# Float32 weighted sums and state products split over two halves of the array's columns, under an order found by a longer search

## The chip, the cores and the metric

The kernel runs on one core of a Trainium2 chip. The metric is the device time of one execution in microseconds (us); lower is better. Engines are named as in the profile: PE is TensorE (its matmuls), PEld its weight loads, DVE is VectorE, ACT is ScalarE, POOL is GpSimd, SP issues most of the DMAs.

## The reference

Attention with a decaying state over 768 tokens, for 4 batches and 8 heads of width 40, then two dense layers with a leaky activation, then three dense layers whose elementwise maximum goes through a last one:

```python
for t in range(S):
    m_new = np.maximum(f_gate[:, :, t] + m, i_gate[:, :, t])
    f_stab = np.exp(f_gate[:, :, t] + m - m_new)
    i_stab = np.exp(i_gate[:, :, t] - m_new)
    C = f_stab * C + i_stab * outer(v_t, k_t)
    n = f_stab * n + i_stab * k_t
    y[:, :, t] = sigmoid(o_t) * (C @ q_t) / np.maximum(np.abs(n @ q_t), 1.0)
...
h = x @ w_in                                   # 3072 x 320 by 320 x 2048
x = (np.maximum(h, 0) + alpha * np.minimum(h, 0)) @ w_out
h = np.maximum(np.maximum(x @ w1, x @ w2), x @ w3)      # 320 x 768 each
return h @ w_out2
```

All data are float32.

## The kernel before

The attention goes by tiles of 128 tokens, 24 in all (`ORDER`). A tile has four products on PE: the scores (`ps`), the weighted sum of the values (`pov`), the product of the queries with the state (`piv`), and the state's own update (`pcv` in `state`, from the 64 columns `kv` and the weighted values `vw`). The state C has 40 rows (on partitions) and 41 columns for each head; the 41st carries n.

Two forms exist. `attention32` works in float32 and serves the 8 tiles for which `whole(p)` holds: six of batch 0 and the first of batches 1 and 2. They are in the first three chunks of three tiles. All others go through `attention`, in pieces of float16; only their state update is in float32. A float32 matmul of the program appears in the profile as two PE instructions. The profile's names: `va` and `db` (or `hl`, where the weights `db` lie in that buffer) are the operands of `pov`; `C` and `q`, `ph` or `hl` (buffers of queries) are those of `piv`; `vw` and `kv` those of the state update.

The dense layers go by 8 chunks of 384 tokens. A unit of the first layer (`m1_unit`) is 8 matmuls of 384 columns (`xT`, `wi`), of the second (`m2_tile`) 12 of 320 (`g`, `wo`) in each of 4 pieces per tile, of the three layers (`m3_unit`) 8 of 384 (`x2T` or `xT`, `wq`), of the last (`m4_tile`) 9 of 320 (`h`, `wp`) in each of 2 pieces. The results are drained from the 8 PSUM banks and split into two float16 parts by DVE, ACT and POOL: after a unit of the first layer ACT writes `d`, DVE `gf`, then two of the three engines write `g`. The weights come as 64-bit floats and are taken apart, measured and converted on chip: their norms are matmuls of 128x128 on PE (from buffer `g` for `w_in`, `wo` and `x2T` for `w_out`, `h` for w1 to w3 in three batches of 15, `wp` for the last), each after a step of DVE that assembles the float32 values, and then the largest goes through `TENSOR_REDUCE dm`, a matmul with `ones`, some steps on DVE, and a conversion of each weight tile (`wo<-wo,sbo` on DVE is the second half of one).

Nothing is issued in the order in which it is written. `Sched` records all operations, and `order` plans them: `forward` simulates the engines by a table of costs (`cost`) and takes on each free engine the ready operation with the earliest due time; `backward` gives new due times from a plan. Where a plan leaves PE idle, it may put in filler matmuls (`ones`, 128x256), which keep the engine active. An operation written with `either` may go to either of two engines. Each engine then runs its list strictly in the planned order, so that an operation that waits holds up all that stands behind it on its engine.

In the code below, line 641 (of before) issues all planned operations, and line 635 the fillers.

Of the kernel before, what the change touches and what calls it, by code (L numbers as in the profile page):

```python
# [51 lines left out]
BY_DMA = 3  # L52

LAG = 4

AFTER = (0, 1, 2, 3)
ROW0 = [sum(CHUNKS[:j]) for j in range(NCH + 1)]
# [85 lines left out]
class Sched:  # L143
# [95 lines left out]
    def cost(self, op, meth, kw, outs, ins):  # L239
        n = 1  # L240
        for x in (ins[0] if meth == "tensor_reduce" else outs[0]).shape[1:]:
            n *= x
        psum = any(a.space == bass.MemoryType.PSUM for a in ins + outs)
        if op.eng == "pe":
            f32 = ins[0].dtype == F32
            wide = kw["lhsT"].shape[1] > 64 if meth == "matmul" else False

            pair = 2 if f32 and ins[0].shape[0] <= 64 else 1
            busy = n * ((4 if meth == "matmul" else 2) if f32 else 1) / 2.4
            if f32 and meth == "matmul":  # L250
                dur = max(busy / pair + 3.5, (214.0 if wide else 107.0) / pair)
            else:
                dur = max(busy + 2.5, 25.0)

            op.weight = (op.weight * op.dur + busy * ins[0].shape[0] / 128.0) / (op.dur + dur)
            op.dur += dur
            lhs = kw["lhsT"] if meth == "matmul" else ins[0]
            op.shape = (ins[0].shape[0] <= 64, lhs.shape[1] <= 64 if meth == "matmul" else False)
        elif op.eng == "act":
            op.dur += n / 1.2 + (60 if psum else 93)  # L260
            if outs[0].shape[0] == 64:
                op.dur += 112
            op.dur += 93 * ("accum_out" in kw)
            op.dur += 93 * sum(hasattr(kw.get(k), "ap") for k in ("scale", "bias"))
        elif op.eng == "dve":
            rate = 0.96
            if meth == "reciprocal":
                rate /= 8
            elif meth in ("tensor_scalar", "tensor_copy", "memset") and not psum:
                rate *= 2  # L270
            if meth == "tensor_tensor_scan":
                rate /= 2
            op.dur += n / rate + 67
            if outs[0].shape[0] == 64 and not psum:
                op.dur += 112
            op.dur += 63 * any(hasattr(kw.get(k), "ap") for k in ("scalar", "scalar1", "scalar2"))
        elif op.eng == "pool":
            op.dur += 100 + ({"affine_select": 1.4, "memset": 1.0}.get(meth, 2.0)) * n
        else:
            b = outs[0]  # L280
            size = SIZE[b.dtype]
            for x in b.shape:
                size *= x
            run = min(self.run(a) for a in (b, ins[0]))
            inside = bass.MemoryType.DRAM not in (b.space, ins[0].space)
            if meth == "dma_start_transpose":
                op.dur += 1290.0
            else:
                op.dur += (590.0 if run < 2048 else 790.0) if inside else 610.0 if b.shape[0] == 64 else 420.0
            n, m = (next((d[1] for d in a.ap if d[1] > 1), 1) for a in (b, ins[0]))  # L290
            k = max(k for k in range(1, 17) if n % k == 0 and m % k == 0)
            slow = run >= 2048 and not (self.level(ins[0]) and self.level(b))
            op.tail = size / run * (self.DMA_EACH + run * (self.DMA_APART if slow else self.DMA_BYTE)) / k
            if meth == "dma_start_transpose":
                op.tail = size / 150.0
# [49 lines left out]
    def order(self):  # L345
        ops = self.ops
        for op in ops:
            op.succ = []
        for i, op in enumerate(ops):
            for d in op.deps:  # L350
                ops[d].succ.append(i)
        best = None
        dice = random.Random(0)

        def walk(due, rounds):
            nonlocal best
            won = None
            for _ in range(rounds):
                plan = self.forward(due)
                if plan is None:  # L360
                    due = [x * 1.01 for x in due]
                    continue
                start, ends, fill = plan
                span = max(ends)
                late = self.backward(start, ends)
                if best is None or span < best[0]:
                    best = (span, start, ends, due, fill, [op.eng for op in ops])
                if won is None or span < won[0]:
                    won = (span, late)
                due = late  # L370
            return won

        from_ = min((w for w in (walk(self.deadlines(*x), ROUNDS) for x in STARTS) if w), key=lambda w: w[0])
        for k in range(SHAKES):
            wide = (12000.0, 4000.0, 1500.0)[k % 3]
            won = walk([x + dice.uniform(-wide, wide) for x in from_[1]], 4)
            if won and won[0] < from_[0]:
                from_ = won
        _, start, ends, due, (self.fill, owner), engs = best
        for bank, n in owner.items():  # L380
            bank.tile = self.tiles[n]
        for op, e in zip(ops, engs):
            if op.forms:
                op.eng, op.calls, op.dur, op.table, op.port = next(f for f in op.forms if f[0] == e)
        self.plan = (start, ends, due)
        return sorted(range(len(ops)), key=lambda i: (start[i], i))
# [266 lines left out]
def kernel(  # L653
# [300 lines left out]
    def attention32(n, xt, t0):  # L954

        b, c = ORDER[n]
        i = b * CT + c
        last = c == CT - 1
        if n % 3 == 0:
            sigmoids(n // 3)  # L960
        t = r_q()
        qt, kt = t[:, 0:4], t[:, 4:8]
        for hh in range(2):
            sp.dma_start(
                out=t[64 * hh:64 * hh + 40].rearrange("p (s h) t -> p s (h t)", s=2),
                in_=qk[i, :, :, 4 * hh:4 * hh + 4, :].rearrange("s p h t -> p s (h t)"),
            )
        gt, db, gm = decays(i)
        kv = r_kv()
        sp.dma_start(out=kv[:, :, 0:DM], in_=tok[i, :, 1:3, :])  # L970
        va = r_va()
        copy(va[:, :, 0:D], kv[:, 1, 0:DM].rearrange("p (h d) -> p h d", d=D))
        ps = [bank("s").rearrange("p (h t) -> p h t", h=4) for _ in range(2)]
        sc.unit()
        for h in range(4):
            for hh in range(2):
                p = slice(64 * hh, 64 * hh + 40)
                pe.matmul(out=ps[hh][:, h, :], lhsT=kt[p, h, :], rhs=qt[p, h, :], start=True, stop=True)
        sc.end()
        for hh in range(2):  # L980
            sl = slice(4 * hh, 4 * hh + 4)
            dve.tensor_tensor(out=db[:, sl], in0=ps[hh], in1=db[:, sl], op=ALU.mult)
        num = r_num() if c else None
        if c:
            cn = carry["C", b]
            piv = [half(bank("a")) for _ in range(2)]
            sc.unit()
            for h in range(4):
                for hh in range(2):
                    p = slice(64 * hh, 64 * hh + 40)  # L990
                    pe.matmul(out=piv[hh][:, h], lhsT=qt[p, h, :], rhs=cn[p, h, :], start=True, stop=True)
            sc.end()
            sc.after(carry["pov"])
            carry["piv"] = len(sc.ops) - 1
            for hh in range(2):
                sl = slice(4 * hh, 4 * hh + 4)
                dve.tensor_tensor(
                    out=num[:, sl], in0=piv[hh], in1=bc(gt[1][:, sl].unsqueeze(2), [128, 4, VA]), op=ALU.mult
                )
        if not last:  # L1000
            vw = r_vw()
            combine(vw, va, bc(gt[2].unsqueeze(2), [128, H, VA]), ALU.mult)
            state(b, c, kv, vw, gm)
        pov = per_head(bank("a"))
        sc.unit()
        for h in range(H):
            pe.matmul(out=pov[:, h], lhsT=db[:, h, :], rhs=va[:, h], start=True, stop=True)
        sc.end()
        if c:
            sc.after(carry["piv"])  # L1010
        carry["pov"] = len(sc.ops) - 1
        if c:
            dve.tensor_tensor(out=num, in0=pov, in1=num, op=ALU.add)
        else:
            num = pov
        finish(n, num, 1.0, xt, t0)
# [513 lines left out]
    for j in range(NCH + LAG):  # L1530
        k = j - LAG
# [63 lines left out]
    (3.0, 30000.0, 1.1),  # L1595
)
ROUNDS = 8
SHAKES = 60
OFFSET = 950.0
STAY = 0.37  # L1600
EARLY = 100000.0
# [50 lines left out]
```

## Time and profile before

| | |
|---|---|
| median of 3 runs | 705.4 us (704.2 to 707.29) |
| the profiled execution: time | 704.88 us |
| its span, first to last instruction | 703.1 us |
| PE busy | 677.5 us, 96% of the span |
| DVE busy | 480.1 us, 68% |
| ACT busy | 392.0 us, 56% |
| mean granted clock of PE | 0.98 of full speed |

A PE that is busy is not a PE at its peak: at half clock it is as busy and does half as much, and the fillers count as well. DVE's 68% is a mean over stretches that differ, so the rows further down are taken by stretch.

### The profile page before, as it was taken

The page shows a single profiled execution, that of the slowest core. Times are in us where ns is not written, and L with a number is a line of the kernel's source. Part 1 is how long each engine was busy: PE and PEld are TensorE (multiplying, and loading weights), DVE is VectorE, ACT ScalarE, POOL GpSimd, SP SyncE. Part 2 cuts the span into 40 slices and gives each one's busy share as a digit, 9 for nine tenths or more (in the row PEclk, how much of TensorE's full clock was granted, in tenths as well). Part 3 has the DMA queues.
Part 4 walks back from the last instruction along what each step waited for, and adds up shares of the span by engine and source line. Part 5 has one row for each costly group of instructions (what it writes and reads, how often), then busy time and mean ns, then how long its engine had stood idle before and what let it go on. Part 6 is the DMA issues. An engine that isn't in the chain of part 4 may idle for free.

```text
span 703.1 us, 14517 instructions
## 1 busy us (share of the span) xinstructions
PE 677.5 (96%) x5353; PEld 456.1 (65%) x5353; DVE 480.1 (68%) x1221; ACT 392.0 (56%) x941; POOL 135.7 (19%) x162
## 2 busy tenths in 40 slices
PE   8898999999999898999999999999999999999998
PEld 5665767667666566666666666666666666666665
DVE  6989889987898989999499835882284214242332
ACT  4778778796986886987376614741253122222222
POOL 1103341131550520442034101410030000000000
PEclk9889799999999999999999999999999999999999
DMA  7978657698744456862624432212101210002000
GB/s 192 281 252 286 220 162 203 203 262 200 206 105 142 139 141 188 268 202 77 184 78 125 128 76 68 70 35 54 52 2 35 35 57 1 29 8 55 10 20 29
DMA packets 81856, 85.76 MB, mean 122 GB/s; under 512 B 38386, under 2 KB 65978, under 8 KB 81786
## 3 DMA queue, kind: packets, MB, share of 16 engines
q1 hardware_dynamic: 81450, 84.77, 42.9%
q8 instruction: 42, 0.69, 0.4%
q14 instruction: 28, 0.23, 0.1%
q10 hardware_dynamic: 336, 0.07, 0.0%
HBM read 59.35 MB, written 8.75 MB: 97 GB/s over the span
## 4 chain that ended last, share of the span: by engine, by line
PE 53%; DVE 5%; ACT 3%; DMA 2%; issue 1%; SPq 1%; ACTq 0%; DVEq 0%
PE bank L641 53%; DVE wq L641 1%; DMA raw<-w 1%; DMA raw<-tok 1%; ACT xs L641 1%; DVE xs L641 1%; SPq L641 1%; DVE g L641 1%; DVE gf L641 0%; ACT wq L641 0%; ACT g L641 0%; ACT raw L641 0%; ACT d L641 0%; DVE num L641 0%; ACT db L641 0%
## 5 line engine op out<-in xcount | busy, mean ns | idle before, releaser
L641 PE MATMUL bank<-xT,wi 128*128 128x384 f16 x1024 | 176.4, 328 | 2.5 <-DVE gf L641 1.6
L641 PE MATMUL bank<-wo,g 128*128 128x320 f16 x1152 | 164.4, 299 | 0.4 <-DVE db L641 0.3
L641 PEld LDWEIGHTS <-wq 128*128 128x128 f16 x1152 | 111.6, 98 | 74.4 <-DVE wq L641 1.6
L641 PEld LDWEIGHTS <-g 128*128 128x128 f16 (+1 forms) x1192 | 114.8, 99 | 47.2 <-DVE g L641 2.4
L641 PEld LDWEIGHTS <-wi 128*128 128x128 f16 x1024 | 98.2, 98 | 65.1 <-issue 5.0
L641 PE MATMUL bank<-x2T,wq 128*128 128x384 f16 x720 | 123.7, 328 | 1.9 <-DVE wq L641 1.2
L641 POOL TENSOR_TENSOR g<-gf,g 128x384 f16<-128x384 f32 x58 | 57.3, 988 | 212.9 <-ACT g L641 140.7
L641 DVE TENSOR_TENSOR mv<-bank,mv 128x384 f32<-128x384 f32 x96 | 53.0, 552 | 62.1 <-PE bank L641 61.7
L641 DVE SCALAR_TENSOR_TENSOR gf<-d,al,bank 128x384 f32<-128x384 f32 x128 | 76.4, 604 | 9.7 <-ACT d L641 8.9
L641 ACT ACTIVATE h<-mv 128x384 f16<-128x384 f32 x46 | 24.0, 522 | 96.1 <-DVE mv L641 96.1
L641 ACT ACTIVATE d<-bank 128x384 f32<-128x384 f32 x128 | 60.7, 479 | 19.3 <-PE bank L641 17.4
L641 PE MATMUL bank<-xT,wq 128*128 128x384 f16 x432 | 71.2, 326 | 0.0
L641 ACT ACTIVATE g<-gf 128x384 f16<-128x384 f32 x104 | 53.6, 518 | 22.2 <-DVE gf L641 21.9
L641 PE MATMUL bank<-wp,h 128*128 128x320 f16 x432 | 61.6, 299 | 0.0
L641 PEld LDWEIGHTS <-h 128*128 128x128 f16 (+1 forms) x477 | 45.7, 98 | 21.2 <-DVE h L641 3.6
L641 ACT ACTIVATE db<-db,gtok 128x128 f32<-128x128 f32 x168 | 54.9, 390 | 0.5 <-POOL db L641 0.4
L641 POOL TENSOR_SCALAR_AFFINE_SELECT db<-db 128x512 f32<-128x512 f32 x42 | 35.0, 849 | 67.5 <-ACT gm L641 52.2
L641 ACT ACTIVATE raw<-raw 128x960 f32<-128x960 f32 (+8 forms) x71 | 44.9, 665 | 2.3 <-DMA raw<-w 1.1
L641 DVE TENSOR_TENSOR g<-gf,g 128x384 f16<-128x384 f32 x70 | 40.8, 588 | 5.8 <-ACT g L641 4.9
L641 POOL TENSOR_TENSOR h<-mv,h 128x384 f16<-128x384 f32 x10 | 9.3, 927 | 167.9 <-ACT h L641 166.1
L641 DVE TENSOR_SCALAR sx<-sx 128x1 int32<-128x1 int32 x48 | 7.1, 147 | 44.6 <-ACT xs L641 44.4
L641 DVE TENSOR_TENSOR h<-mv,h 128x384 f16<-128x384 f32 x38 | 21.1, 556 | 18.1 <-ACT h L641 17.9
(209 smaller groups left out, 797.9 us busy)
## 6 DMA issues: line engine op xcount, KB each, us to landing
db<-ddr SPq DMA_DIRECT2D x21, 512.0 KB
kv<-tok SPq DMA_DIRECT2D x24, 320.0 KB
raw<-tok SPq DMA_DIRECT2D x15, 480.0 KB
q<-qk SPq DMA_DIRECT2D x38, 160.0 KB
raw<-w SPq DMA_DIRECT2D x9, 512.0 KB
qs<-hl SPq DMA_DIRECT2D x48, 80.0 KB
x2d<-xs SPq DMA_DIRECT2D x24, 160.0 KB
ks<-hl SPq DMA_DIRECT2D x48, 80.0 KB
```

The source lines that it names most:

```text
L641: getattr(e, meth)(**{k: v.on(v.bank.tile) if isinstance(v, View) else v for k, v in kw.items()})
```

## The change

In `attention32`, each matmul of `piv` and `pov`, which had 128 columns of weights (the tile's 128 tokens), becomes two of 64 columns, for tokens 0 to 63 and 64 to 127, one after the other. Their results go to partitions 0 to 63 and 64 to 127 of the same bank. The state update already had this form (64 columns, the two halves in turn) and is left alone, as are the scores.

In the planner, `cost` gets another price for float32 matmuls (with 64 columns of weights the price is now for halves that run beside each other; this is also the state update's, of 20 tiles). `order` compares plans by their span plus a fifth of the mean start, and each of now 200 further attempts moves the due times of the best plan so far within one stretch, for one round, instead of 60 attempts over the whole program for four rounds.

```diff
+HALVES = (slice(0, 64), slice(64, 128))
...
-            pair = 2 if f32 and ins[0].shape[0] <= 64 else 1
+            pair = 1
+            if f32 and meth == "matmul":
+                pair = (1 + (ins[0].shape[0] <= 64)) * (1 + (kw["lhsT"].shape[1] <= 64))
...
-                dur = max(busy / pair + 3.5, (214.0 if wide else 107.0) / pair)
+                dur = max(busy / pair + 3.5, kw["lhsT"].shape[1] * 1.67 / pair + 6.0)
...
-                if best is None or span < best[0]:
+                worth = span + 0.2 * sum(start) / len(start)
+                if best is None or worth < best[0]:
...
-            wide = (12000.0, 4000.0, 1500.0)[k % 3]
-            won = walk([x + dice.uniform(-wide, wide) for x in from_[1]], 4)
+            won = walk([x + dice.uniform(-wide, wide) if a <= x < b else x for x in from_[1]], 1)
...
-                for hh in range(2):
-                    p = slice(64 * hh, 64 * hh + 40)
-                    pe.matmul(out=piv[hh][:, h], lhsT=qt[p, h, :], rhs=cn[p, h, :], start=True, stop=True)
+                for t in HALVES:
+                    for hh in range(2):
+                        p = slice(64 * hh, 64 * hh + 40)
+                        pe.matmul(out=piv[hh][t, h], lhsT=qt[p, h, t], rhs=cn[p, h, :], start=True, stop=True)
...
-            pe.matmul(out=pov[:, h], lhsT=db[:, h, :], rhs=va[:, h], start=True, stop=True)
+            for t in HALVES:
+                pe.matmul(out=pov[t, h], lhsT=db[:, h, t], rhs=va[:, h], start=True, stop=True)
...
-SHAKES = 60
+SHAKES = 200
```

The new plan moves instructions on every engine. (Line 647 of the changed kernel issues what line 641 did, and its line 641 the fillers.) Three places show how.

PE, around the norm of `w_out` (`dm`, `ones` 128x4) and the first unit of the second layer (`wo`, `g`); first before, from the last of the norms that this step waits for:

```order
L641 MATMUL bank_67<-x2T 128x128
L641 MATMUL bank_69<-va_138,db_135 128x41 x8
L641 MATMUL bank_66<-vw_141,kv_133 64x41 x8
L641 MATMUL bank_63<-ph_142 128x128
...
L641 MATMUL bank_64<-C_145,ph_142 128x41
...
L641 LDWEIGHTS ones
L641 MATMUL bank_67<-dm_164,ones 128x4
L641 LDWEIGHTS wi_90
L641 MATMUL bank_69<-xT_110,wi_90 128x384
```

And the same place in the changed kernel, to the first unit of the second layer:

```order
L647 MATMUL bank_64<-x2T 128x128
L647 LDWEIGHTS ones
L647 MATMUL bank_64<-dm_164,ones 128x4
L641 LDWEIGHTS ones
L641 MATMUL bank_69<-ones 128x256
...
L647 MATMUL bank_69<-vw_141,kv_134 64x41 x8
L647 MATMUL bank_70<-va_138,db_136 64x41 x16
...
L647 LDWEIGHTS g_105
L647 MATMUL bank_66<-wo_92,g_105 128x320
```

The four float32 groups that stood between the norms and the step `dm`, `ones` now stand ahead of the norms; behind that step, 13 fillers stand where four units of the first layer (`xT`, `wi`) were mixed with the float32 groups.

DVE, just ahead of the reduction that this step needs, first before:

```order
L641 CAST g_107<-gf_118 128x384
L641 SCALAR_TENSOR_TENSOR gf_119<-d_117,al_75,bank_69 128x384
L641 TENSOR_TENSOR db_135<-bank_66,db_135 128x512
L641 TENSOR_TENSOR db_135<-bank_63,db_135 128x512
L641 TENSOR_TENSOR num_143<-bank_68,gtok 128x164
L641 TENSOR_TENSOR num_143<-bank_64,gtok 128x164
L641 TENSOR_REDUCE dm_164<-bank_67 128x4
```

and then in the changed kernel:

```order
L647 SCALAR_TENSOR_TENSOR gf_119<-d_117,al_75,bank_70 128x384
L647 TENSOR_TENSOR C_145<-bank_63,C_145 128x164
L647 TENSOR_SCALAR dn_152<-num_143 128x8
...
L647 TENSOR_TENSOR g_108<-gf_119,g_108 128x384
L647 TENSOR_TENSOR y_144<-num_143,dn_152 128x320
L647 TENSOR_REDUCE dm_164<-bank_64 128x4
```

The reduction was DVE's 177th instruction and is now its 190th: steps of the first layer's units and of one attention tile (`num`, `dn`, `y`) have moved ahead of it.

PE, in the second batch of norms for w1 to w3 (`h`), where before seven of them stand together behind a weighted sum:

```order
L641 MATMUL bank_67<-vh_139,ph_142 128x41
L641 LDWEIGHTS h_109
L641 MATMUL bank_68<-h_109 128x128
...
L641 LDWEIGHTS wq
L641 MATMUL bank_69<-x2T,wq 128x384
```

and in the changed kernel the last of the same batch:

```order
L647 LDWEIGHTS h_109
L647 MATMUL bank_65<-h_109 128x128
L647 LDWEIGHTS wi_89
L647 MATMUL bank_64<-xT_111,wi_89 128x384
...
L647 LDWEIGHTS h_109
L647 MATMUL bank_65<-h_109 128x128
L647 LDWEIGHTS wq
L647 MATMUL bank_68<-x2T,wq 128x384
```

In the second and third batch the norms now stand one by one, each with a unit or half a unit of other work behind it.

## Rows read from the trace of the kernel before

**Rows 1.** The page: busy time of each engine, share of the span, instructions.

```profile
PE 677.5 (96%) x5353; PEld 456.1 (65%) x5353; DVE 480.1 (68%) x1221; ACT 392.0 (56%) x941; POOL 135.7 (19%) x162
```

**Rows 2.** Busy time by stretch: from:to, length, then each engine, clock, DMA.

```profile
0.00:98.10 98.10, 85.16 (x730) 63.67 (x730) 82.68 (x219) 70.02 (x154) 19.94 (x38) 0.88 0.78 235
98.10:353.10 255.00, 245.84 (x2132) 167.09 (x2131) 221.99 (x593) 199.26 (x510) 76.12 (x83) 0.99 0.64 180
353.10:703.10 350.00, 346.50 (x2493) 225.30 (x2492) 175.47 (x411) 122.76 (x279) 39.68 (x42) 1.00 0.18 48
```

**Rows 3.** The chain that ended last: start, us, what.

```profile
352.62 0.48 DVE dm L641
353.14 346.51 PE bank L641 x2493
```

**Rows 4.** Timeline of PE, 60 to 99 us: start, length, instruction.

```profile
62.32 1.09 PE L641 MATMUL bank<-C,ph 40*128 40x41 f32 x16
63.34 1.47 PE L641 MATMUL bank<-xT,wi 128*128 128x384 f16 x8
64.74 0.67 PE L641 MATMUL bank<-vw,kv 128*64 128x41 f32 x16
65.34 1.98 PE L641 MATMUL bank<-va,db 128*128 128x41 f32 x16
67.15 0.23 PE L641 MATMUL bank<-wo 128*128 128x128 bf16 x1
67.22 1.46 PE L641 MATMUL bank<-xT,wi 128*128 128x384 f16 x8
68.52 0.22 PE L641 MATMUL bank<-wo 128*128 128x128 bf16 x1
...
79.85 3.58 PE L641 MATMUL bank<-va,db 128*128 128x41 f32 x16
83.36 1.08 PE L641 MATMUL bank<-vw,kv 128*64 128x41 f32 x16
...
86.24 1.77 PE L641 MATMUL bank<-C,ph 40*128 40x41 f32 x16
87.95 0.19 PE L641 MATMUL bank<-dm,ones 128*128 128x4 bf16 x1
...
98.10 0.58 PE L641 MATMUL bank<-wo,g 128*128 128x320 f16 x3
```

**Rows 5.** Busy time in two stretches of low granted clock, columns as in rows 2.

```profile
77.50:91.50 14.00, 14.00 (x113) 12.04 (x113) 9.87 (x27) 9.60 (x26) 4.84 (x7) 0.51 0.51 151
...
240.00:256.00 16.00, 13.67 (x118) 8.62 (x116) 13.76 (x34) 14.00 (x42) 5.11 (x6) 0.89 0.60 158
```

**Rows 6.** Timeline of DVE between the reduction and the first converted weights.

```profile
80.09 0.69 DVE L641 TENSOR_REDUCE dm<-bank 128x4 bf16<-128x512 f32 x1 [0.42 <-PE bank L641]
...
88.33 0.15 DVE L641 TENSOR_SCALAR xm<-bank 128x4 int32<-128x4 int32 x1
...
91.67 0.33 DVE L641 TENSOR_TENSOR C<-bank,C 128x164 f32<-128x164 f32 x1 [0.80 <-PE bank L641]
...
94.77 0.50 DVE L641 TENSOR_TENSOR num<-bank,num 128x328 f32<-128x328 f32 x1 [0.61 <-PE bank L641]
...
96.15 0.87 DVE L641 SCALAR_TENSOR_TENSOR wo<-wo,sbo,wo 128x640 f16<-128x640 f32 x1
```

**Rows 7.** Timeline of PE at the second batch of norms.

```profile
241.59 0.76 PE L641 MATMUL bank<-vh,ph 128*128 128x41 f16 x24
242.20 0.27 PE L641 MATMUL bank<-h 128*128 128x128 bf16 x2
243.47 0.23 PE L641 MATMUL bank<-h 128*128 128x128 bf16 x1 [0.99 <-DVE h L641]
245.03 0.61 PE L641 MATMUL bank<-h 128*128 128x128 bf16 x4 [1.34 <-DVE h L641]
```

**Rows 8.** The state update's weight loads: count, busy us, mean ns, idle.

```profile
L641 PEld LDWEIGHTS bank<-vw,kv 128*64 128x64 f32 x320 | 11.6, 145 | 6.3 <-issue 3.3 <-DVE sx L641 1.1 <-POOL vw L641 0.7
```

More of the change, by code (lines that the diff above doesn't have):

```diff
@@ L245, in cost @@
             f32 = ins[0].dtype == F32
-            wide = kw["lhsT"].shape[1] > 64 if meth == "matmul" else False
-            pair = 2 if f32 and ins[0].shape[0] <= 64 else 1
+            pair = 1
+            if f32 and meth == "matmul":
+                pair = (1 + (ins[0].shape[0] <= 64)) * (1 + (kw["lhsT"].shape[1] <= 64))
             busy = n * ((4 if meth == "matmul" else 2) if f32 else 1) / 2.4
             if f32 and meth == "matmul":
-                dur = max(busy / pair + 3.5, (214.0 if wide else 107.0) / pair)
+                dur = max(busy / pair + 3.5, kw["lhsT"].shape[1] * 1.67 / pair + 6.0)
             else:
@@ L365, in walk @@
                 late = self.backward(start, ends)
-                if best is None or span < best[0]:
-                    best = (span, start, ends, due, fill, [op.eng for op in ops])
-                if won is None or span < won[0]:
-                    won = (span, late)
+                worth = span + 0.2 * sum(start) / len(start)
+                if best is None or worth < best[0]:
+                    best = (worth, start, ends, due, fill, [op.eng for op in ops])
+                if won is None or worth < won[0]:
+                    won = (worth, due)
                 due = late
@@ L374, in order @@
         for k in range(SHAKES):
-            wide = (12000.0, 4000.0, 1500.0)[k % 3]
-            won = walk([x + dice.uniform(-wide, wide) for x in from_[1]], 4)
+            end = max(from_[1])
+            a = dice.uniform(-0.05, 0.95) * end
+            b = a + dice.choice((20000.0, 60000.0, 150000.0, 800000.0))
+            wide = dice.choice((500.0, 1500.0, 4000.0, 12000.0))
+            won = walk([x + dice.uniform(-wide, wide) if a <= x < b else x for x in from_[1]], 1)
             if won and won[0] < from_[0]:
```

## The prediction

> **What bounds the kernel now.** I read the busy times first, then the chain that ended last, then the same busy times by stretch, cut where the chain and PE's timeline say that the limit changes. PE is busy for 96% of the span [rows 1], which looks like one bound for the whole program. The chain says otherwise: from 353.1 us on it is PE alone, 2493 matmuls in 346.5 us without a break, and just before that it runs over DVE, whose step `dm` is the measure of the last weights [rows 3]. So I divide the span in three [rows 2].
>
> Stage A, 0 to 98.1 us, ends with the first unit of the second layer [rows 4]. PE is busy for 85.2 of 98.1 us, part of it with fillers and part at half clock; DVE is busy for 82.7. Stage B, 98.1 to 353.1 us, ends with the matmul behind that last `dm`. PE is busy for 245.8 of 255.0 us and idle for 9.2, DVE is busy for 222.0 and ACT for 199.3: PE is the nearest bound, DVE a close second. Stage C, 350 us, is PE's alone; DVE is busy for half of it, and nothing that DVE, ACT or the DMAs save there can show. The sum is made against the profiled execution: 704.9 us, of which the span is 703.1; that is 0.5 us below the median of 705.4, and I forecast on the execution's scale. About 0.5%, 3.5 us, is what a measurement of this kernel can tell from no change: below 701.9 I call it faster, above 708.9 slower.
>
> **The matmuls that are split.** One `pov` is 16 instructions in 65.34 to 67.15 us, 1.81 us at full clock. The new one is 32 instructions of the very form of the state update (128 rows, 64 columns of weights, 41 moving columns, float32, halves in turn), which takes 16 instructions from 64.74 to 65.34, 0.60 us [rows 4]. Twice that is 1.20 us, so each `pov` gives 0.61 us. `piv` is 16 instructions in 1.02 us (62.32 to 63.34). With 40 rows and 64 columns four pieces of the array could work at once, a form that the trace does not have. At the pitch of the state update, 37.5 ns, 32 instructions would be 1.20 us, a loss of 0.18; at the shortest pitch I find, 24 float16 matmuls of the same 41 columns in 0.61 us, 25.4 ns each [rows 7], they would be 0.81 us, a gain of 0.21. I take nothing, as the middle.
>
> Counted in the order, 6 of the 8 `pov` and 4 of the 5 `piv` stand in stage A before and after the change; 2 and 1 stand in stage B. None is in stage C. So of the whole 8 x 0.61 = 4.9 us only 1.2 us lies where PE is the bound; the other 3.7 us lie in stage A and count only if what ends stage A comes earlier. The price of a change of form, when PE goes from whole columns to halves, is seen at the state update: the unit ahead of it takes 1.40 us (63.34 to 64.74) where another takes 1.30 (67.22 to 68.52), so 0.10 us. The order has 12 more such changes, all of them in stage A; in stages B and C the count stays at 32. They are hidden with the rest of stage A; without that cover they would cost 1.2 us.
>
> **A rule that speaks against the split.** The 16 weight loads and matmuls of a state update start 37.5 ns apart though a load takes 145 ns on average [rows 4, 8], so loads and matmuls of the two column halves do overlap. The Trainium skill, "TensorE: Matmul & The Clock Gate", section "The mechanism", says that a weight load overlaps with running matmuls only when its row group differs; the two halves here have the same rows. By that rule the split would gain nothing; the trace's state update disagrees, and I go by the trace.
>
> **The end of stage A.** The first unit of the second layer waits for converted weights, and these for a chain: norms on PE, the reduction on DVE, a matmul with `ones` on PE, steps on DVE, the conversion. Before, the reduction starts at 80.09 us [rows 6], but the matmul behind it only at 87.95, since 8.1 us of float32 groups stand ahead of it on PE (79.85 to 87.95), all of them at half clock [rows 4, 5]: a `pov` takes 3.51 us there, a state update 1.01. DVE goes on at 88.33, and converts the second weight tile from 96.15 to 97.02 [rows 6]; PE starts the unit at 98.10.
>
> In the new order nothing stands between the norms and the matmul with `ones`, so these 8 us of waiting are gone. Instead 13 more instructions stand ahead of the reduction on DVE. At the stage's mean, 82.7 us for 219 [rows 2], they are 4.9 us; by their kinds (five `gf`, three `g` and small ones) I count 5.9. The reduction then starts at 86.0, ends at 86.7, and DVE goes on some 0.4 us later at 87.1, 1.2 us earlier than before. From there to the conversion DVE took 7.8 us, 1.4 of it waiting for PE's slow float32 groups (0.80 and 0.61 [rows 6]); with half of that wait gone, the conversion starts 1.9 us earlier. PE has 13 fillers and 5 us of float32 work to do meanwhile, so it is ready. I take 1.9 us off stage A. The bounds: a gain of 6.9 us, if all that the low clock took from 77.5 to 91.5 us comes back (14.0 us at a mean of 0.51 of full speed [rows 5]); and a loss of 1.5 us, if DVE waits in front of the reduction for the attention steps that now stand there, as long as the 1.4 us that it waited behind it.
>
> **Stage B and C.** Counted by the order, two units of the first layer (2.6 us) move from C to B, and the two split `pov` take 1.2 us off B; the two stages together lose 1.2 us of PE work. In B, PE's clock fell to half at the second batch of norms: two waits of 0.99 and 1.34 us for DVE within 3 us, among single matmuls [rows 7], and of the 16 us there 11% of the clock was lost [rows 5], 1.8 us of work. In the new order the norms of that batch and the next stand one by one between units, so such waits no longer fall together. I take the 1.8 us off, and leave the 9.2 us of idle time as it is: the new order has other waits in the place of these, and which is larger no row tells. The bounds are 0 and all of 9.2 us.
>
> SP issues as many DMAs as before, no wait of PE in stage B is for a DMA, and the state update, whose price in the planner halves, is not itself changed: there I expect nothing.
>
> The sum: -1.9 (A) -1.2 (split, B) -1.8 (clock, B) = -4.9, so 704.9 - 4.9 = 700.0 us.
>
> **Rivals.** *DVE holds up stage B (slower).* Between the conversion at the end of stage A and the last `dm`, DVE has 607 instructions where it had 596. The 11 more are wide ones, splits and scalings that went to ACT or POOL before; by kind I count 6.2 us (4.1 at the mean of 222.0 us for 593 [rows 2]). PE has 1.4 us more there. If DVE keeps its share of waiting, stage B grows with it: 255.0 x (6.2 / 222.0) = 7.1 us. Less the 1.9 of A and the 2.6 us that left C, that is +2.6: 707.5 us; it is slower than before from 4.5 us of added DVE time that finds no gap. Against it: DVE is idle for 33 us of stage B, and PE, not DVE, is nearest to full. Slower by more than 0.5% takes a further 1.4 us.
>
> *The waits of stage B go (much faster).* If the longer search fits DVE's work so that PE hardly waits, the 9.2 us go too: 700.0 - 9.2 = 690.8. For it speaks the new price of the state update: a head cost 107 ns in the old plan and 59 in the new one, where it takes 75 (0.60 us for 8 heads [rows 4]), so PE ran ahead of the old plan, into waits, and falls behind the new one. Against it: the planner meant the old stage B to be nearly free of waits as well (it placed two fillers there, as now), and the 9.2 us came all the same.
>
> *Nothing but the two splits counts.* The gate of stage A comes no earlier (the 5.9 us on DVE are matched by waits), and the clock falls elsewhere instead: 704.9 - 1.2 = 703.7.
>
> *The halves do not overlap.* 32 loads at 145 ns [rows 8] are 4.6 us where a `pov` took 1.81: 2.8 us each, 5.7 in stage B alone and up to 22.6 in all, 711 to 727 us. Only a difference between `pov` and the state update that I do not see could bring it; this is what the rule of the skill above comes to.
>
> **How the numbers follow.** 0.38 for the forecast (its own range 697 to 703), 0.17 for the waits that go (690 to 697), 0.24 for nothing but the splits (703 to 706), 0.19 for DVE (706 to 711), 0.02 for halves that do not overlap. The likeliest is 700.0. Leaving out some 0.08 at the low end and 0.10 at the high end gives 693 to 708.5. Faster by over 0.5%: 0.17 and 0.31 of the forecast's 0.38 below 701.9, so 0.48. Slower: 0.02 and 0.15 of DVE's 0.19, so 0.17. The rest, 0.35, is no change that can be told.
>
> **What would show it.** A `pov` of 32 instructions in 1.2 us, a `piv` near 1.0. The reduction `dm` 128x4 at about 86 us, the matmul behind it at once, the first unit of the second layer at about 96. Between that and the last `dm`, PE's idle time: 9 us bears the forecast out, 14 and more, with waits for DVE, the rival; a granted clock of 1.00 from 240 us on. From the last `dm` to the end, 2.6 us less than 350. Wrong would make it above all a stretch of half clock in the new stage A or B that the old order did not have, since 13 fillers in a row show that the plan itself has PE waiting there.

## The result and the profile after

The changed kernel takes 695.96 us (695.4 to 696.97, 4 runs) where the kernel before, on the same chip, took 705.15: a ratio of 0.9867, 95% interval [0.9842, 0.9893], so 9.2 us less. Single executions far off the others of their kernel (2093 and 2401 us below, 714 and 728 us of the kernel before) are in no ratio of this document. The changed kernel's profiled execution has a span of 694.1 us, 9.0 less than 703.1. Cut at the same two places as before (the first `wo`, `g`, and the matmul behind the last `dm` 128x3), its busy times by stretch are these; columns as in [rows 2]:

```profile
0.00:91.10 91.10, 72.89 (x886) 51.17 (x887) 79.68 (x213) 68.00 (x152) 18.45 (x37) 0.94 0.85 248
91.10:345.50 254.40, 246.72 (x2193) 166.80 (x2191) 227.16 (x611) 199.89 (x517) 67.02 (x76) 0.99 0.65 183
345.50:694.10 348.60, 344.32 (x2483) 223.89 (x2480) 172.48 (x405) 120.95 (x273) 40.81 (x45) 1.00 0.17 48
```

Beside [rows 2], stage A is 7.0 us shorter (98.1 to 91.1), stage B 0.6, stage C 1.4. So 7.0 of the 9.0 us, over three quarters, lie in the stage where the forecast had put 1.9 of 4.9. The granted clock of A rose from 0.88 to 0.94. Before, it stood at half (1.2 of 2.4 GHz) from 29.9 us for 10.2 us, from 77.7 for 13.7, and in B from 244.9 for 3.4. Now, in this execution, it falls five times, but never for more than 3.4 us; the same view, cut at these falls and at the place of [rows 5]:

```profile
22.00:25.50 3.50, 3.30 (x26) 2.66 (x27) 2.10 (x8) 2.19 (x6) 0.15 (x1) 0.51 1.04 281
39.20:42.60 3.40, 2.98 (x18) 2.04 (x18) 3.35 (x14) 2.59 (x7) 0.00 (x0) 0.50 0.97 312
83.50:86.90 3.40, 3.26 (x22) 2.18 (x21) 2.23 (x11) 3.40 (x9) 0.00 (x0) 0.51 0.74 212
158.60:162.00 3.40, 3.40 (x32) 2.45 (x29) 3.19 (x10) 3.28 (x8) 0.00 (x0) 0.51 0.42 108
240.00:256.00 16.00, 15.28 (x125) 10.72 (x126) 15.62 (x39) 13.87 (x41) 4.04 (x5) 1.00 0.62 156
315.60:319.00 3.40, 3.40 (x17) 1.66 (x14) 2.88 (x10) 1.56 (x6) 0.00 (x0) 0.51 0.56 195
```

The fall at 240 to 256 us is gone, as forecast; those at 158.6 and 315.6 are new. In all of stage A the clock stands at half for 10.2 us where it was 23.9. PE's timeline around the end of stage A, which answers to [rows 4] (start, length, instruction):

```profile
74.17 0.68 PE L647 MATMUL bank<-C,q 40*64 40x41 f32 x32
74.78 0.23 PE L647 MATMUL bank<-wo 128*128 128x128 bf16 x1
...
77.65 1.13 PE L647 MATMUL bank<-va,db 128*64 128x41 f32 x32
78.72 0.23 PE L647 MATMUL bank<-wo 128*128 128x128 bf16 x1
...
80.90 0.68 PE L647 MATMUL bank<-C,ph 40*64 40x41 f32 x32
81.51 0.35 PE L647 MATMUL bank<-x2T 128*128 128x128 bf16 x3
83.64 0.17 PE L647 MATMUL bank<-dm,ones 128*128 128x4 bf16 x1 [1.78 <-DVE dm L647]
83.66 2.94 PE L641 MATMUL bank<-ones 128*128 128x256 bf16 x13
...
91.10 1.11 PE L647 MATMUL bank<-wo,g 128*128 128x320 f16 x7
```

From its start to the start of what follows, a split `pov` takes 1.07 us (77.65 to 78.72) for its 32 instructions, a split `piv` 0.61 (74.17 to 74.78): both shorter than forecast (1.20 and 1.02). The float32 groups that stood behind the norms now run at full clock, and ahead of the last of these. Behind the step `dm`, `ones` come the 13 fillers, as the order showed. DVE's timeline, which answers to [rows 6]:

```profile
82.91 0.68 DVE L647 TENSOR_REDUCE dm<-bank 128x4 bf16<-128x512 f32 x1
...
87.42 0.33 DVE L647 TENSOR_TENSOR C<-bank,C 128x164 f32<-128x164 f32 x1 [1.66 <-PE bank L647]
```

The reduction starts at 82.91 us and the matmul behind it 0.73 us later (before: 80.09, and 7.86 later). From the reduction to the first unit of the second layer it is now 8.2 us, and was 18.0.

One more row of the kernel before is needed, its busy time from the wait at 75.98 us to the end of stage A; columns as in [rows 2]:

```profile
75.98:98.10 22.12, 22.12 (x196) 18.51 (x196) 17.21 (x53) 15.46 (x39) 6.49 (x9) 0.69 0.53 157
```

PE is busy for all of these 22.12 us, at 0.69 of full speed, and DVE for 17.21. So the first unit of the second layer did not wait for the converted weights: it began when PE was through with what stood ahead of it. There, time taken off PE's work brings the end of stage A forward, for as long as PE does not come to wait.

### The profile page after: what moved, and what is told of

Read it like the earlier page. It is cut to its first block, busy times and chain, and to the rows that moved or that the text cites. A ratio compares the mean times of both kernels' runs of the same rounds, so it can differ in the third digit from the quotient of the medians.

```text
span 694.1 us, 14964 instructions
## 1 busy us (share of the span) xinstructions
PE 663.9 (96%) x5558; PEld 441.9 (64%) x5558; DVE 479.3 (69%) x1227; ACT 388.8 (56%) x940; POOL 126.3 (18%) x157
## 4 chain that ended last, share of the span: by engine, by line
PE 57%; DVE 5%; ACT 1%; issue 1%; DVEq 0%; ACTq 0%
PE bank L647 57%; DVE gf L647 1%; DVE db L647 1%; DVE ph L647 0%; DVE g L647 0%; ACT db L647 0%; DVE wp L647 0%; DVE num L647 0%; DVE y L647 0%; DVE h L647 0%; DVE dn L647 0%; DVE vh L647 0%; DVE wq L647 0%; DVE xs L647 0%; ACT xs L647 0%
## 5 line engine op out<-in xcount | busy, mean ns | idle before, releaser
L647 PE MATMUL bank<-xT,wi 128*128 128x384 f16 x1024 | 174.6, 326 | 2.3 <-DVE db L647 1.4
L647 POOL TENSOR_TENSOR g<-gf,g 128x384 f16<-128x384 f32 x54 | 52.9, 984 | 206.7 <-ACT g L647 144.6
L647 ACT ACTIVATE g<-gf 128x384 f16<-128x384 f32 x111 | 57.2, 519 | 16.3 <-DVE gf L647 15.7
L647 DVE TENSOR_TENSOR g<-gf,g 128x384 f16<-128x384 f32 x74 | 43.8, 600 | 10.2 <-ACT g L647 9.4
L647 ACT ACTIVATE raw<-raw 128x512 f32<-128x512 f32 (+8 forms) x70 | 44.6, 655 | 4.0 <-DMA raw<-tok 2.6
L647 POOL TENSOR_TENSOR h<-mv,h 128x384 f16<-128x384 f32 x15 | 13.7, 913 | 178.3 <-ACT h L647 173.6
L647 POOL TENSOR_SCALAR_AFFINE_SELECT db<-db 128x512 f32<-128x512 f32 x42 | 31.1, 761 | 80.3 <-ACT gm L647 57.8
L647 ACT ACTIVATE mv<-bank 128x384 f32<-128x384 f32 x35 | 17.0, 487 | 30.1 <-PE bank L647 30.1
L647 ACT ACTIVATE xs<-bank 128x320 f16<-128x320 f32 x24 | 10.3, 429 | 40.7 <-PE bank L647 40.4
```

The lines of the kernel that those rows point to most:

```text
L647: getattr(e, meth)(**{k: v.on(v.bank.tile) if isinstance(v, View) else v for k, v in kw.items()})
```

## The experiments

Two theories stood against each other. *The order* (P in the expectations): stage A is shorter since the new plan puts the float32 groups ahead of the norms; the split is hidden there. *The split and the clock* (S): stage A is shorter since split groups end sooner or no longer run at half clock, whatever the order. A third question is what in the planner made the plan better: the price, the longer search, or chance. The kernels ran in three groups, each on a chip of its own, where the kernel before had medians of 706.6 to 708.4 us; so ratios to it are compared, and stages from the one profiled execution of each. The profiled execution of the kernel before took 704.9 us, 1.7 to 3.5 us less than these medians, so stages show less gain than ratios.

**The changed kernel again** (no edit), for the spread.

> The changed kernel itself, unchanged, beside the next three on one chip, so that they can be held against it: ratio to before 0.987, as in the first comparison (0.984 to 0.989); stage A 91, stage B 254, stage C 349 us.

Measured: 696.57 us, ratio 0.9849 [0.9818, 0.9880]. Stages A, B and C are 92.8, 251.4 and 349.1 us where the first profile has 91.1, 254.4 and 348.6. So one stage of one profile is uncertain by 2 to 3 us, from half clock that falls at other places (here 20.5, 75.1, 85.3 and 160.4 us).

**The split alone, in the old order.** The plan of before is kept word for word (it is made with whole matmuls); only at issue are the halves taken:

```diff
-            for meth, kw in op.calls:
+            for meth, kw in getattr(op, "other", op.calls):
...
+            sc.ops[-1].other = [
+                ("matmul", dict(out=piv[hh][t, h], lhsT=qt[64 * hh:64 * hh + 40, h, t], rhs=cn[64 * hh:64 * hh + 40, h, :], start=True, stop=True))
+                for h in range(4) for t in HALVES for hh in range(2)
+            ]
...
+        sc.ops[-1].other = [
+            ("matmul", dict(out=pov[t, h], lhsT=db[:, h, t], rhs=va[:, h], start=True, stop=True))
+            for h in range(H) for t in HALVES
+        ]
```

> The order of before, kept word for word on every engine (planned with whole matmuls), but pov and piv are issued in halves. Measured in the changed kernel, a split pov takes about 1.0 us and a split piv 0.6, where they took 1.8 and 1.0. Theory P (the new order pays, the split alone counts only where PE is the bound): two pov and one piv stand in stage B, so about -2.0 us, stage A ends at 98 as before: ratio 0.997. Theory S (the split pays by itself, since the float32 groups from 79.9 to 98 us, half of them at half clock, also stood in front of the step dm, ones): pov 3.5 to 2.0, piv 1.7 to 1.2, and 0.8 and 0.4 for the two at full clock, so stage A ends 3 us earlier as well: -5 us, ratio 0.993; if the clock no longer falls there, up to -9.

Measured: 700.61 us, ratio 0.9894 [0.9872, 0.9917]. Its busy time by stretch, the first two stages:

```profile
0.00:90.70 90.70, 74.72 (x890) 53.10 (x890) 82.00 (x218) 69.29 (x152) 19.15 (x37) 0.94 0.83 255
90.70:347.90 257.20, 244.80 (x2182) 164.85 (x2181) 222.60 (x595) 199.92 (x512) 75.74 (x84) 0.99 0.65 179
```

Stage A is 7.4 us shorter with the old order; theory P had expected nothing there, and theory S 3 us. Its PE timeline there, in the same order as [rows 4]:

```profile
76.83 1.94 PE L643 MATMUL bank<-va,db 128*64 128x41 f32 x32
78.53 1.01 PE L643 MATMUL bank<-vw,kv 128*64 128x41 f32 x16
79.47 1.16 PE L643 MATMUL bank<-ph 40*128 40x128 f32 x16
80.81 0.68 PE L643 MATMUL bank<-C,ph 40*64 40x41 f32 x32 [0.17 <-DVE C L643]
81.42 0.18 PE L643 MATMUL bank<-dm,ones 128*128 128x4 bf16 x1
...
90.74 1.80 PE L643 MATMUL bank<-wo,g 128*128 128x320 f16 x12
```

The clock falls at the same place of the program (75.9 us here, 77.7 before), but comes back after 3.4 us and not after 13.7. The four float32 groups ahead of `dm`, `ones` take 4.6 us (76.83 to 81.42) and took 8.1. In stage B the split gains nothing in this profile: PE is busy for 1.0 us less and idle for 3.2 more (12.4 where it was 9.2), so that B is 2.2 us longer, which is within the 2 to 3 us by which a stage is uncertain.

Where the 7.4 us come from can be read off step by step, since DVE runs the same list in both kernels. At DVE's 81st step they differ by 0.1 us (33.84 and 33.73), at its 93rd by 2.2 (40.40 and 38.22). Between these stands one `pov` at half clock, first before, then split:

```profile
33.11 3.64 PE L641 MATMUL bank<-va,hl 128*128 128x41 f32 x16 [0.27 <-ACT va L641]
33.07 1.94 PE L643 MATMUL bank<-va,hl 128*64 128x41 f32 x32
```

To the start of what follows it takes 3.43 us and 1.87, so at half clock the split takes 1.56 us off a `pov`, twice as much as at full clock (0.74). The 2.2 us stay until the last norms of `w_out`; 0.8 more are there at the reduction, and 4.4 come behind it. From the wait ahead of these norms to the first unit of the second layer it is now 16.94 us (22.12 before):

```profile
73.80:90.74 16.94, 15.36 (x277) 11.95 (x277) 16.06 (x53) 14.96 (x38) 6.09 (x8) 0.90 0.67 199
```

**The order alone, with whole matmuls**: the same device the other way round, the plan of the changed kernel with whole matmuls at issue.

```diff
+        sc.ops[-1].other = [
+            ("matmul", dict(out=pov[:, h], lhsT=db[:, h, :], rhs=va[:, h], start=True, stop=True))
+            for h in range(H)
+        ]
```

> The order of the changed kernel, kept on every engine, but pov and piv are issued whole, as before. Theory P (the order pays): about +2.0 us on the changed kernel's 696.0, the two pov and one piv of stage B, so 698, ratio to before 0.990. Theory S (the split pays): stage A ends later too, by the float32 groups just ahead of and behind the step dm, ones (0.4 and 0.8, 0.4 us at full clock), and by more if the clock falls there again: 700 to 703, ratio 0.994 to 0.998.

Measured: 704.5 us, ratio 0.9957 [0.9927, 0.9988]; stages 96.5, 255.0 and 348.6 us. DVE's reduction and PE's next step, from its two timelines:

```profile
86.38 0.68 DVE L647 TENSOR_REDUCE dm<-bank 128x4 bf16<-128x512 f32 x1
...
87.11 0.16 PE L647 MATMUL bank<-dm,ones 128*128 128x4 bf16 x1 [1.05 <-DVE dm L647]
```

Stage A is 1.6 us shorter in this profile, of an execution of 701.84 us. The ratio is what theory S expected. The two parts add up: 1.06% for the split (0.83 to 1.28 by its interval), 0.43% for the order (0.12 to 0.73), together 1.49%, and the whole change 1.33% and 1.51% in its two comparisons.

**The clock alone, in the old order with whole matmuls.** PE waits 1.75 us for the last tile of `w_out` just ahead of the fall at 77.7; 16 fillers are put there:

```diff
+    sc.fill[held] = (16, min(free_, key=lambda n: last_[n]))
```

> The kernel before with 16 more filler matmuls (1.7 us) in the gap of 1.75 us in front of the norms of the last tile of w_out at 76 us, and nothing else. If the half clock from 77.7 to 91.3 us is what held up stage A, and the gap brought it, the clock stays at full speed there, the first unit of the second layer starts at 92 to 94 us instead of 98.1, and the time falls by 4 to 6 us (ratio 0.992 to 0.994). If DVE's chain sets the end of stage A anyway, or the clock falls all the same through the float32 groups, it changes by less than 1 us.

Measured: 701.28 us, ratio 0.9899 [0.9882, 0.9915]. PE's timeline:

```profile
75.40 1.91 PE L635 MATMUL bank<-ones 128*128 128x256 bf16 x16
...
80.34 1.95 PE L641 MATMUL bank<-va,db 128*128 128x41 f32 x16
...
94.67 1.80 PE L641 MATMUL bank<-wo,g 128*128 128x320 f16 x12
```

and its busy time over the place of the fall, clock in the third column from the end:

```profile
75.40:90.00 14.60, 14.12 (x168) 11.73 (x166) 14.27 (x45) 12.73 (x36) 5.07 (x7) 1.00 0.82 240
77.30:94.67 17.37, 16.41 (x197) 13.43 (x197) 17.04 (x53) 15.24 (x39) 6.04 (x9) 1.00 0.71 203
```

With the clock at 1.00 the same `pov` takes 1.88 us and not 3.51. From DVE's reduction (80.64) to the first unit of the second layer it is 14.0 us; before it was 18.0, and with the split 13.6 (77.11 to 90.74). So with the clock alone 4.0 of the split's 4.4 us come back in that stretch; from the last norms of `w_out` to that unit it is 17.37 us (second row), 4.8 less than before, with the split 5.2. The total time is as good as with the split, and better than was expected (0.992 to 0.994). This profile's stage A is only 3.4 us shorter, since the clock fell elsewhere ahead of this stretch (for 13.7 us at 25.7 and for 3.4 at 56.4).

**Split, but the halves not in turn**: first all heads of tokens 0 to 63, then of 64 to 127. In `piv` the two row halves, which stood in turn before, are drawn apart as well.

```diff
-            for h in range(H) for t in HALVES
+            for t in HALVES for h in range(H)
```

> The changed kernel with the same 64-column matmuls of pov and piv, but all heads of tokens 0 to 63 first and then all of 64 to 127, so that neighbours use the same half of the columns. If the split gains because the two halves work beside each other, a pov goes back to 1.8 us or more (32 loads, no overlap between neighbours) and the time rises by 2 us or more, to 698 or above. If a 64-column load is simply half as long and overlaps with anything, a pov stays near 1.0 us and the time at 696.

Measured: 702.57 us, ratio 0.9905 [0.9882, 0.9928]. PE's timeline, a `pov` and a `piv`:

```profile
68.30 1.85 PE L647 MATMUL bank<-va,db 128*64 128x41 f32 x32
70.08 1.47 PE L647 MATMUL bank<-xT,wi 128*128 128x384 f16 x8
...
75.89 1.44 PE L647 MATMUL bank<-C,q 40*64 40x41 f32 x32
77.26 0.23 PE L647 MATMUL bank<-wo 128*128 128x128 bf16 x1
```

The same 32 instructions take 1.78 us where they took 1.07, and 1.37 where they took 0.61. So what makes a split `pov` or `piv` itself shorter is that neighbours lie in different parts of the array. Without that a `pov` gains nothing (1.81 whole) and a `piv` loses 0.35 (1.02 whole, with its rows in turn). That the two halves of a `pov` share their moving columns is not what does it: the state update's neighbours share none, and start 37.5 ns apart.

But the kernel as a whole does not fall back to the order alone. In the same order and on the same chip, whole matmuls gave 0.9957 [0.9927, 0.9988] and these, which are no shorter, 0.9905 [0.9882, 0.9928]. The intervals just touch. So some 0.5% of the split's 1.06% does not need shorter matmuls. It goes with the clock: over the runs behind these ratios the mean granted clock is 0.983 to 0.990 here and 0.969 to 0.983 with whole matmuls. In its profile it did not fall at all around the end of stage A:

```profile
70.00:96.00 26.00, 23.91 (x338) 19.12 (x337) 24.55 (x70) 22.12 (x53) 5.84 (x8) 1.00 0.72 228
```

**What in the planner carries the order's part.** Four kernels change the planner alone: the new price with the old search, the old price with the new search, and either search from another start of the random numbers (`Random(1)` for `Random(0)`).

> The changed kernel with the new prices of float32 matmuls, but the search of before (60 attempts over the whole program, plans compared by span alone). If the gain of the order over the old one (about 4 us against the old order with split matmuls) comes from the longer search, this plan gives 0.990 to 0.993 to before, as the old order with split matmuls did (0.989); if it comes from the prices, 0.987 as the changed kernel.

> The changed kernel with the old prices (107 ns for any float32 matmul with 64 columns of weights, half of it with 40 rows) and the new search. If the search makes the order better, 0.985 to 0.988; if the prices do, 0.990 or above. In either case a pov takes about 1.0 us, since the matmuls are the split ones.

> The changed kernel with another seed of the search's random numbers (1 in place of 0) and nothing else. If the order's part of the gain is what the new search reaches as a rule, the time stays within 0.3% of the changed kernel's; if it is the luck of one plan, it lies anywhere between 0.982 and 0.995 to before.

> The split matmuls and new prices with the old search, as in e5_new_price_old_search, but with seed 1 of the random numbers. If the prices are what makes the order better, 0.980 to 0.988 again; if that run's 0.981 was the luck of one plan, 0.988 or above.

| split, planned with | ratio to before | span, stages A + B + C |
|---|---|---|
| new price, new search (the change, again) | 0.9849 [0.9818, 0.9880] | 693.4 = 92.8 + 251.4 + 349.1 |
| new price, old search | 0.9809 [0.9766, 0.9852] | 695.0 = 90.4 + 259.1 + 345.6 |
| old price, new search | 0.9916 [0.9891, 0.9942] | 703.4 = 92.7 + 260.4 + 350.3 |
| new price, new search, other start | 0.9829 [0.9788, 0.9870] | 690.0 = 87.2 + 254.7 + 348.1 |
| new price, old search, other start | 0.9708 [0.9670, 0.9745] | 684.7 = 87.4 + 253.4 + 343.9 |

With the old price, 200 attempts of the new search give no more than the split in the old order (0.9894). (Its profile is of an execution of 706.0 us, 5 above its median.) With the new price all four plans are better than that, and the old search isn't worse than the new one. That speaks for the price, but two plans of the old price stand against four of the new, and another start alone changes a time by up to 1.1% (0.9809 and 0.9708), so it is not settled. One of the old search's two plans, 686.65 us, is the best kernel here, 1.4% below the changed one and outside of what was expected for it either way; its clock falls only once, for 3.4 us at 33.9, and its stage A is 87.4 us long:

```profile
0.00:87.40 87.40, 72.60 (x907) 51.37 (x908) 79.86 (x206) 69.44 (x157) 23.86 (x41) 0.98 0.84 255
```

Of the 9.4 us by which its span is below the changed kernel's, 3.7 lie in stage A and 4.7 in stage C, where PE has 4.4 us less to do (339.95 us and 344.32): more of its work stands ahead of the last `dm`.

**The new price without the split**: the kernel before, planned with the new price (which then changes the state update's alone).

> The kernel before, matmuls whole and with its own search, but with the new prices: a state update's matmul costs 59 instead of 107, a whole pov's 220 instead of 214, a whole piv's 113 instead of 107. If the order's part of the gain comes from the state update's price (20 tiles, 8 heads each: 7.7 us of PE time that the old plan reckoned with and the chip does not spend), the ratio to before is 0.988 to 0.994 without any split. If the better order needs the short pov and piv, it stays at 0.996 to 1.004.

Measured: 703.53 us, ratio 0.9948 [0.9915, 0.9980]; stages 93.5, 255.7 and 350.9. That lies between the two expectations: the price is worth about what the order alone was (0.9957), and the split is needed for the rest. (Of the 7.7 us that the expectation calls not spent, 2.6 are: a state update's matmul takes 75 ns, between the prices of 107 and 59.) Its clock stands at half for 17.1 us from 47.1 on.

**The 13 fillers behind `dm`, `ones`.** One kernel leaves them out, one has 16 ahead of that step in their place.

```diff
+    assert sc.fill[behind][0] == 13
+    del sc.fill[behind]
```

> The changed kernel without the 13 fillers behind the step dm, ones (1.4 us of work at full clock), and nothing else. If they only fill a wait for DVE, the time stays within 0.2% of the changed kernel's 0.985 to 0.987. If they are what brings the clock back, the half clock that begins at 83 to 85 us lasts on through the float32 groups and the first units of the second layer (in the kernel before it lasted 13.7 us at this place): stage A or the start of stage B takes 2 to 5 us more, 0.989 to 0.993.

> The changed kernel with the 13 fillers moved: 16 fillers ahead of the step dm, ones, where PE waits 1.8 us for DVE, none behind it. If the fall to half clock at 83.5 us follows from that wait, as it did in the kernel before the norms of w_out, it does not come, stage A ends 1 to 2 us earlier: 0.982 to 0.985. If the fall follows from the float32 groups and the norms ahead of the wait, the clock falls all the same and, with nothing dense behind, stays low longer: 0.988 or above.

Measured: 0.9830 [0.9790, 0.9869] without them, 0.9860 [0.9818, 0.9901] with fillers ahead: neither can be told from the changed kernel. Busy time of the kernel without them and of the changed kernel over the same time (the reduction is at 84.5 us in the one, at 82.9 in the other):

```profile
83.00:94.00 11.00, 8.49 (x138) 7.10 (x139) 10.78 (x34) 8.88 (x21) 1.26 (x2) 0.60 0.65 178
```

```profile
83.00:94.00 11.00, 9.60 (x133) 7.26 (x133) 9.27 (x32) 8.29 (x21) 0.47 (x1) 0.84 0.65 173
```

Without fillers the clock stays at half for 10.2 us from 85.1 on, and next to nothing comes of it: from the reduction to the first unit of the second layer it is 8.7 us, with the fillers 8.2 and 8.25 in the changed kernel's two profiles. DVE is busy for 10.78 of 11 us, and PE waits for it at either clock. With fillers ahead, the fall at 83.5 is gone, but the clock falls at 86.7 for 6.8 us, behind three waits for DVE of 0.98, 0.31 and 0.29 us; neither of its two expectations came. So what a stretch of half clock costs differs with what PE would otherwise wait for: 10.2 us of it in place of 3.4 cost about 0.5 us here, and the 13.7 us of the kernel before, in which PE had no gap, 4 to 5 us by the run with the 16 fillers.

## Why the prediction was right, and where it was not

The sign and the range held (693 to 708.5), and the forecast of 700.0 was 4 us too high. That the range held is in part luck: the measured time lies where the forecast had put the rival that the waits of stage B go (690 to 697), and it came there by stage A. The sign that was to show the forecast wrong above all, half clock at places where the old order had none, appeared in A and B, and the time fell all the same. The chances do not fit together: 0.10 is left above 708.5, but 0.17 is given to times above 708.9. By its steps:

- **The split** was undersized. A `pov` gives 0.74 us (1.81 to 1.07) and not 0.61, a `piv` 0.41 (1.02 to 0.61) and not nothing. The rival that halves do not overlap is false for the order in the code; when the halves are not in turn the gain is gone, but a `pov` still takes 1.78 us and not the rival's 4.6. The Trainium skill, "TensorE: Matmul & The Clock Gate", section "The mechanism", has it that a weight load overlaps running matmuls only where the row group differs. The traces disagree: all instructions of a split `pov` use the same rows, and 32 loads of 138 ns and their matmuls start within 1.07 us; with the same matmuls in another order, neighbours in one column half, they take 0.71 us more.
- **The end of stage A** is the step that failed: -1.9 forecast, -7.0 measured. What it priced, the order, came out near it in the one profile that has it alone: with whole matmuls the reduction came at 86.38 (forecast 86.0) and stage A lost 1.6 us. What failed is the path. The forecast let the first unit wait for converted weights and so for a chain over DVE, and of the split it said "the other 3.7 us lie in stage A and count only if what ends stage A comes earlier", and counted nothing. But before, PE had no gap for the last 22.12 us of stage A, at a mean clock of 0.69, so that its own work set the end, and the 3.7 us were too small as well, being taken at full clock. The split brought the end forward in the old order by 7.4 us, more than the 6.1 us of array time that it takes off stage A at full clock (6 x 0.74 and 4 x 0.41). Of these 7.4, 2.2 come at the first stretch of half clock, 1.56 of them in one `pov`; 0.8 come between the last norms and the reduction, and 4.4 behind it. Fillers alone, which keep the clock up, give 0.8 and 4.0 in these last two places. My bound for this, a gain of 6.9 "if all that the low clock took from 77.5 to 91.5 us comes back", was near the right number, and I gave it no case of its own. The wait of DVE that was to halve did not: it was 0.80 and 0.61 us, and is 1.66 in one piece now.
- **The clock in stage B**, -1.8, failed. The fall at the norms went, but two new ones came, at 158.6 behind waits of 0.89 and 0.51 us for DVE, and at 315.6 behind one of 2.27. At 0.51 each takes 1.7 us of work. In the second profile of the same kernel only the first of the two came (at 160.4), though the wait of 2.3 us was there too, so that such a wait does not settle whether the clock falls. PE's row for the second in the first profile, with the wait in brackets:

```profile
315.10 0.67 PE L647 MATMUL bank<-vw,kv 128*64 128x41 f32 x16 [2.27 <-DVE vw L647]
```

- **The split in stage B**, -1.2, was no gain that showed by itself: in the old order it turned into waiting (B +2.2). With the new order B lost 0.6 us though it has more work; the forecast had 0.4 (two units more, 2.6, less 1.2 and 1.8). So B came near its sum by luck: the terms were not met, and the second profile has 251.4 us for it.
- **Stage C** lost 1.4 us and not 2.6. PE has 2.2 us less to do there, and 0.86 us went into one wait for DVE (`wp`, at 359.95).
- **The rival of DVE** had its premise right: DVE works 227.2 us in B where it worked 222.0, 5.2 more (6.2 counted). It found gaps: PE's idle time in B fell from 9.2 to 7.7 us. The rival that the waits of B go did not come either. The one that nothing but the two splits counts had the clock falling elsewhere; that did happen, in B, and in A for 10.2 us where it was 23.9.

Open is why the half clock ended after 3.4 us with split groups and lasted 13.7 through whole ones, while PE was busy in both. The longest stretch of half clock was 13.7, 13.7, 13.7 and 17.1 us in the four kernels with whole matmuls, and 3.4 to 10.2 in the nine with split ones. Over the runs behind the ratios, the mean granted clock averages 0.977 to 0.980 in the kernels with whole matmuls, but for the one with the 16 fillers (0.987), and 0.983 to 0.994 in those with split ones, also where the halves are not in turn and the groups no shorter (0.987). So the length of the groups alone is not what does it. It is a pattern; the cause is not shown.

## What to carry to other kernels

Before a gain on PE is called hidden behind a chain over other engines, look whether PE has a gap ahead of the place where the stage ends, and at what clock it runs there. Where it has none and the clock is at half, shortening its work, or keeping the clock up by a few fillers in the wait just ahead of the fall, can be worth more than its time at full clock says (16 fillers gave 1.0% here, as much as the split; at a place where PE waits for DVE they gave nothing). Split matmuls are themselves shorter only in turn, half beside half. When a planner's price is mended, try several starts of its search before making the search longer: plans of the same price differed by up to 1.4%, and the longer search was better from neither of its two starts.

## What the runs showed of the hardware

Float32 matmuls of 40 rows and 64 columns of weights, on four parts of the array in turn, started 19 ns apart on average (32 in 0.61 us), and 43 ns when neighbours shared a part (1.37 us); those of 128 rows in two column halves 33 ns apart, and 56 ns when neighbours shared a half. So one and the same set of matmuls, of 41 moving columns each, took 1.7 to 2.2 times as long by the order of its neighbours. And the kernel before itself varied from 702.0 to 711.7 us on these chips, with a mean granted clock of 0.990 at the lower end and 0.976 at the upper: the spread of one kernel goes in the main with how long PE stands at half clock. PE could be busy without a gap and stay at half: for 13.7 us from 77.7 in the kernel before.
